# A linear-recurrence attention followed by a PReLU layer: second part block by block, states per 64 tokens, one buffer split, and a static plan with new durations

## The chip, the cores and the metric

One core of a Trainium2 chip. The metric is the device time of one execution in microseconds (us), as the median of the timed runs.

## The reference, cut to what matters

```python
# part 1: batch 4, heads 8, sequence 768, head size 48; for each (b, h):
mag = sqrt(a_re**2 + a_im**2);  scale = minimum(mag, 0.999) / (mag + 1e-6)
for t in range(768):                        # complex decay, real input
    S = (a_re + 1j * a_im)[t, :, None] * scale * S + k[t][:, None] * v[t]
    y[t] = (q[t][:, None] * S.real).sum(0)
# part 2: x is y with the heads side by side, (3072, 384)
h = x @ w_in                                # 384 -> 2048
g = maximum(h, 0) + alpha * minimum(h, 0)
out = g @ w_out                             # 2048 -> 384
```

The first part is done in 24 units of 128 tokens (6 per batch), all heads together. Inside a unit, pairs of tokens are met by levels: the level of h multiplies the second h tokens of each stretch of 2h by the first h. What reaches a unit from earlier tokens comes through a state.

## The kernel before

The program's order of instructions is fixed while it is built. Each piece of work is a generator that yields steps (engine, estimated duration, what it waits for, which buffers it takes). A small planner runs the generators against these durations and puts out the instructions in the order in which they would start. The tasks have dates: a unit of attention is due at `DUE_0 + RATE * u`, the first gates run between `G0`, `G1` and `G2`, the weights are spread from `W_FROM` to `W_TO`. On the chip each engine follows that order, and where an instruction is not ready the engine waits.

```python
class Plan:
    HOP, DRAIN, SLACK, LAND, RATE = 0.06, 0.2, 0.4, 2.0, 200.0
    ...
            now = min(t for t, _ in ready) + 0.3      # choice window
            t, task = min(((t, k) for t, k in ready if t <= now), key=lambda x: (not x[1][1][5], x[1][2]))

R = {name: Ring(n) for name, n in dict(               # buffers of the plan
    KQ=3, PP=1, T=2, V=2, W=2, KT=1, St=2, yT=1, xT=2, g=3, ot=2, wtmp=1,
    lv=2, misc=1, y=1, h=2, o=1).items()}             # the last row is PSUM
sizes = [1, 1] + [MC] * ((NU - 4) // MC) + [1, 1]     # blocks of part 2, in 128 tokens; MC = 2

def mlp(m):                                           # one block of part 2
    for f in range(NF):                               # 16 groups of 128 features
        for kk in range(NK):                          # 3 products
            e = yield PE(n * 1.68e-3, ("x", m), ("w_in", f), takes=() if kk else (R["h"],))
            if kk == 0:
                p = ps.tile([P, MT], F32, tag="h", name="ps_h", bufs=2)[:, 0:n]
            nc.tensor.matmul(p, lhsT=w_in_sb[:, kk, f * P:(f + 1) * P], rhs=xT[:, kk], ...)
        ...                                           # ScalarE: relu, VectorE: + alpha part
    for c in range(sizes[m]):                         # then all outputs, one 128 tokens at a time
        for f in range(NF):
            if f == 0:
                p = ps.tile([P, DM], F32, tag="o", name="ps_o")
            nc.tensor.matmul(p, lhsT=G[f][:, cols], rhs=w_out_sb[:, f], ...)

def to_f32(dst, parts, scales, *key):                 # weights arrive as 64-bit floats
    ta = yield ACT(n, ("raw", *key), takes=(R["wtmp"],))
    tmp = work.tile([P, 2] + list(dst.shape[1:]), F32, tag="wtmp", name="wtmp", bufs=1)
    top, rest = tmp[:, 0], tmp[:, 1]
    ...                                               # 2 ScalarE, 5 VectorE steps
    for i, r in enumerate(parts):                     # ps_w: identity products add top and rest
        ...
    R["wtmp"].put(e)

def half_rows():                                      # v re-sorted by level, in DRAM
    for i, h in enumerate(KINDS):
        for n in range(HP):
            ...
            nc.sync.dma_start(dst, src)               # outermost count of src: 64 / h per unit

# in unit(): levels 1, 2, ... 64, then one state per unit
LEVELS = [1 << i for i in range(7)]
...
t = ps.tile([D2, H, D], F32, tag="misc", name="ps_kv")
for n in range(H):
    nc.tensor.matmul(t[:, n], lhsT=KT[:, n], rhs=V[:, n // 2, ...], ...)
```

`D2` is 96 (real and imaginary part of 48), `P` is 128 and `HC` is 64. PSUM is full in both kernels. With each tile in pieces of 2 KB per partition to itself, the tiles take eight: before, lv 2, misc 1, y 2, h 2, o 1; after, lv 2, misc 1, y 2, h 1, o 2. The Trainium skill, "PSUM — Partial Sum Buffer", section "PSUM: the matmul accumulator", gives eight banks of 2 KB. In this change the second output tile is paid for by joining the two tiles of ps_h into one.

Of the kernel before, what the change touches and what calls it, by code (L numbers as in the profile page):

```python
# [15 lines left out]
P = 128  # L16
# [19 lines left out]
class Plan:  # L36
# [4 lines left out]
    HOP = 0.06  # L41
    DRAIN = 0.2
    SLACK = 0.4
    LAND = 2.0
    RATE = 200.0

    def __init__(self):
        self.busy, self.done, self.tasks = {}, {}, []

# [7 lines left out]
    def _ready(self, e, engine):  # L57

        if e[1] in (engine, None):
            return e[0]  # L60
        return e[0] + self.HOP + self.DRAIN * (e[1] == "PE") + self.SLACK * (engine == "PE")

# [16 lines left out]
    def run(self):  # L79
        while self.tasks:  # L80
# [5 lines left out]
            now = min(t for t, _ in ready) + 0.3  # L86
# [17 lines left out]
def kernel(  # L104
# [46 lines left out]
    LEVELS = [1 << i for i in range(7)]  # L151
# [51 lines left out]
    def POOL(n, *after):  # L203
        return "POOL", 0.12 + n * 1.9e-3, after, (), 0, False

    def PE(us, *after, takes=()):
        return "PE", us, after, takes, 0, False

    def DMA(kb, *after, takes=(), engine="SP"):
# [3 lines left out]
        KQ=3, PP=1, T=2, V=2, W=2, KT=1, St=2, yT=1, xT=2, g=3, ot=2, wtmp=1,  # L213
        lv=2, misc=1, y=1, h=2, o=1).items()}
# [12 lines left out]
    nc.gpsimd.memset(decays_sb[:, :, TL - 1], 0.0)  # L227

    def gates(b, c0, c1):
# [6 lines left out]

        def small(k, *after):

            return POOL(k, *after) if k <= SMALL else DVE(k, *after)

        def on(k):
            return nc.gpsimd if k <= SMALL else nc.vector
# [56 lines left out]
        for o, (p, w) in enumerate(((y, -1.0), (x, 1.0), (y, 1.0))):  # L299
            tu = yield ACT(2 * N, tx, t)  # L300
            nc.scalar.activation(U3[:, o], p.rearrange("p (n l) -> p l n", l=L), AF.Copy, scale=w)  # L301
        at = 0
        while at < TL - 2:
# [20 lines left out]
        def product(dst, u, w, m, k, t):  # L324

            m = m[:, 0:4 * k].rearrange("p (a c n) -> p a c n", a=2, c=2)
            yield small(2 * k, t)
            on(2 * k).tensor_tensor(out=m, in0=w[:, 1::-1].unsqueeze(2).to_broadcast([P, 2, 2, k]), in1=pairs_of(u), op=ALU.mult)  # L328
# [25 lines left out]
        def three(dst, re_im, t):  # L354

            yield ACT(re_im.free_size(), t)
            nc.scalar.copy(dst[:, 1:3], re_im)
            t = yield ACT(re_im.free_size() // 2, t)
            nc.scalar.activation(dst[:, 0], re_im[:, 1], AF.Copy, scale=-1.0)
            return t  # L360
# [6 lines left out]
        t = yield POOL(10, t)  # L367
        if first:
            nc.gpsimd.memset(run[:, 0, :, 0], 1.0)
            nc.gpsimd.memset(run[:, 1, :, 0], 0.0)  # L370
        else:
            nc.gpsimd.tensor_copy(run[:, :, :, 0], carry)
# [3 lines left out]
        if not last:  # L376
            yield POOL(10, t)
            nc.gpsimd.tensor_copy(carry, run[:, :, :, nr])
# [6 lines left out]
        for o in range(2):  # L385
            yield POOL(2 * k, t)
            nc.gpsimd.tensor_tensor(out=m, in0=blk[:, :, 0:Rn - 1],
               in1=turned(runs, o).unsqueeze(2).to_broadcast([P, 2, Rn - 1, rows]), op=ALU.mult)
            t = yield POOL(k)
            nc.gpsimd.tensor_tensor(out=offv[:, o, 1:Rn], in0=m[:, 0], in1=m[:, 1], op=ALU.add)  # L390
# [4 lines left out]
        yield POOL(nb, t)  # L395
        nc.gpsimd.tensor_tensor(out=n2[:, 0], in0=n2[:, 0], in1=n2[:, 1], op=ALU.add)
        yield POOL(nb)
        nc.gpsimd.tensor_scalar(out=n2[:, 0], in0=n2[:, 0], scalar1=-0.5, scalar2=1.5, op0=ALU.mult, op1=ALU.add)
        t = yield POOL(2 * nb)
        nc.gpsimd.tensor_tensor(out=off, in0=off, in1=n2[:, 0].unsqueeze(1).to_broadcast([P, 2, nb]), op=ALU.mult)  # L400
# [59 lines left out]
    def to_f32(dst, parts, scales, *key):  # L460

        n = 2 * DM
        ta = yield ACT(n, ("raw", *key), takes=(R["wtmp"],))
        raw = raws.pop(key)
        lo, hi = raw[:, :, :, 0], raw[:, :, :, 1]
        tmp = work.tile([P, 2] + list(dst.shape[1:]), F32, tag="wtmp", name="wtmp", bufs=1)
        top, rest = tmp[:, 0], tmp[:, 1]
        top_u, dst_u = top.bitcast(U32), dst.bitcast(U32)
        nc.scalar.activation(top, hi.bitcast(F32), AF.Abs)
        tl = yield ACT(n, ta)  # L470
        nc.scalar.activation(rest, lo, AF.Copy, scale=2.0 ** -52)

        yield DVE(n // 2, ta)
        nc.vector.tensor_scalar(out=top, in0=top, scalar1=F64_SMALL, scalar2=None, op0=ALU.max)

        yield DVE(n // 2)
# [7 lines left out]
        yield DVE(n // 2)  # L484
# [3 lines left out]
        nc.vector.tensor_tensor(out=rest, in0=rest, in1=top, op=ALU.mult)  # L488
        for i, r in enumerate(parts):
# [9 lines left out]
        R["wtmp"].put(e)  # L499
# [102 lines left out]
    def unit(u):  # L602
# [18 lines left out]
        def mask_out(name, t, n, e):  # L621

            takes = (R[name],)
            if name in by_row or name == HC:
                e = yield ACT(HP * n if name == HC else HP * name + 100, e, takes=takes)
# [4 lines left out]
            if name == HC:  # L630
                nc.scalar.copy(a, t)
            elif name in by_row:
# [49 lines left out]
        for h in LEVELS[1:-1]:  # L682
# [11 lines left out]
        h = HC  # L694
        e, t = yield from meet(h, lambda n: KQ[:, 1, n, 0:HC], second(h), HC, k_, q_)

        if c + 1 < NCH:
            k_ = yield DVE(H * HC, e)
            step(1, h)
        if c:  # L700
            q_ = yield DVE(H * HC, e)
            step(0, h)
        yield from mask_out(h, t, HC, e)


        before, known = state.pop(b, (None, None))
        if c + 1 < NCH:
            for i in range(2):
                e = yield PE(0.34, k_, takes=(R["misc"],))
                t = ps.tile([P, HP, D2], F32, tag="misc", name="ps_kt")  # L710
                for p in range(4):
                    nc.tensor.transpose(t[:, p], KQ[:, 1, 4 * i + p], ident[:D2, :D2])
                e = yield ACT(HP * D2, e, takes=() if i else (R["KT"],))
                if i == 0:
                    KT = work.tile([P, H, D2], F32, tag="KT", name="KT", bufs=1)
                nc.scalar.copy(KT[:, 4 * i:4 * i + 4], t)
                R["misc"].put(e)
            e = yield PE(1.32, e, ("V", u), takes=(R["misc"],))
            V = L["V"]
            t = ps.tile([D2, H, D], F32, tag="misc", name="ps_kv")  # L720
            for n in range(H):
                nc.tensor.matmul(t[:, n], lhsT=KT[:, n], rhs=V[:, n // 2, (n % 2) * D:(n % 2 + 1) * D],  # L722
                                 start=True, stop=True)
            R["KT"].put(e)
            if before is None:
                s_ = yield ACT(H * D, e, takes=(R["St"],))
                St = work.tile([D2, H, D], F32, tag="St", name="St", bufs=2)
                nc.scalar.copy(St, t)
            else:
                s_ = yield DVE(H * D, known, takes=(R["St"],))  # L730
                St = work.tile([D2, H, D], F32, tag="St", name="St", bufs=2)
                nc.vector.tensor_tensor(out=St, in0=before, in1=T[:, :, TL - 2:TL - 1].to_broadcast([D2, H, D]),
                                        op=ALU.mult)
                s_ = yield DVE(H * D, e)
                nc.vector.tensor_tensor(out=St, in0=St, in1=t, op=ALU.add)
            R["misc"].put(s_)
            state[b] = St, s_
            R["T"].put(s_)
        else:
            R["T"].put(q_)  # L740

        g, cg = group_of[u]
        for s in range(2):
            for part in range(2):
                names = [("own", 0), ("own", 1)] + [(h, 0) for h in LEVELS]
                e = yield PE(0.58, ("V", u), *(made if not (s or part) else ()),
# [5 lines left out]
                for name, own in names[5 * part:5 * part + 5]:  # L752
                    for e_ in range(2):
                        for i in range(2):
# [6 lines left out]
                                             start=(name == "own" and not own), stop=(name == HC and c == 0))  # L761
            if c:
                e = yield PE(0.58, q_, known)
                for i in range(2):
# [148 lines left out]
```

## Time and profile before

| | before |
|---|---|
| time, median of 4 runs (range) | 1106.28 us (1105.12 to 1107.64) |
| span of the profiled run, mean granted clock of TensorE | 1103.6 us, 0.895 |
| first matmul of part 2 | 227.5 us |
| end of the weights' conversion (start of its last product) | 237.7 us |
| last attention product (ps_y) | 998.7 us |

TensorE is the busiest engine by far, so I keep its account throughout as **lost time**: at time t, t minus what all matmuls issued by then would last at full speed. Durations at full speed come from dense stretches of the traces: ps_h 0.220 us for 256 tokens and 0.110 for 128, ps_o 0.324, ps_lv 0.038, ps_y 0.0155, ps_w 0.324, ps_kt 0.083, a ps_kv of whole height 0.083 and of 64 rows 0.047, a state product 0.072 and with half the columns 0.032. Lost time is idle time and low clock together, and is good to about 2 us. Before, the work is 792 us and 312 us are lost by the end of the span.

### The profile page before, as it was taken

What the parts mean: (1) busy time and instruction counts of PE and PEld (TensorE: products, weight loads), DVE (VectorE), ACT (ScalarE), POOL (GpSimd) and SP (SyncE); (2) the same over time, 40 slices, a digit from 0 to 9 for tenths busy, and PEclk for the clock granted to TensorE, in tenths of its full rate; (3) what the DMA queues carried; (4) which work ended last, traced back from release to release, by engine and by line L of the source; (5) the groups of instructions that cost most, each with busy time, mean ns of one, the idle gap of its engine ahead of it and who ended that gap; (6) DMA issues with size and microseconds to landing.
All of it is one profiled execution on the core that took longest, in us unless ns stands there. A gap on an engine that the chain in (4) does not pass through costs nothing.

```text
span 1103.6 us, 23784 instructions
## 1 busy us (share of the span) xinstructions
PE 921.2 (83%) x9952; PEld 647.9 (59%) x9952; DVE 731.6 (66%) x1114; ACT 501.2 (45%) x949; POOL 145.2 (13%) x367
## 2 busy tenths in 40 slices
PE   1453675599978888998897999998989999999998
PEld 0121343376757566676476666685666666877676
DVE  5376789667966587677765877697658765761122
ACT  4362664365625464465244634562546342442122
POOL 5113002400050004000310031003100320000000
PEclk9556667599969899998988999999989989999999
DMA  5784789069726880686338664945393339501000
GB/s 165 207 186 125 174 216 277 7 171 169 172 93 166 180 215 22 191 169 140 119 120 159 157 154 120 216 108 144 127 203 77 97 101 171 133 10 30 7 15 15
DMA packets 210179, 147.05 MB, mean 133 GB/s; under 512 B 71704, under 2 KB 201880, under 8 KB 210072
## 3 DMA queue, kind: packets, MB, share of 16 engines
q1 hardware_dynamic: 210072, 145.53, 54.5%
q8 instruction: 78, 1.28, 0.5%
q14 instruction: 29, 0.24, 0.1%
HBM read 117.19 MB, written 47.97 MB: 150 GB/s over the span
## 4 chain that ended last, share of the span: by engine, by line
PE 60%; DVE 14%; ACT 8%; POOL 7%; issue 5%; SPq 3%; DMA 2%; DVEq 0%; ACTq 0%; POOLq 0%
PE ps_o L829 21%; PE ps_h L810 18%; PE ps_lv L617 6%; PE ps_y L759 5%; POOL tmp L328 3%; PE ps_kv L722 2%; POOL blk L330 2%; DVE tmp L328 2%; PE ps_y L767 2%; SPq L544 2%; DVE KQ L679 2%; PE ps_lv L660 2%; DVE g L818 2%; ACT tmp L301 2%; ACT g L816 2%
## 5 line engine op out<-in xcount | busy, mean ns | idle before, releaser
L810 PE MATMUL ps_h<-xT,w_in_sb 128*128 128x256 f32 (+1 forms) x1344 | 302.4, 373 | 18.7 <-issue 10.7
L829 PE MATMUL ps_o<-w_out_sb,g 128*128 128x384 f32 x768 | 279.9, 505 | 1.8 <-ACT ot L835 1.8
L810 PEld LDWEIGHTS ps_h<-xT,w_in_sb 128*128 128x128 f32 x1344 | 227.5, 197 | 63.4 <-DVE g L818 21.3
L679 DVE TENSOR_TENSOR KQ<-KQ,T 96x512 f32<-96x512 f32 x280 | 191.6, 693 | 81.7 <-PE ps_lv L617 51.3
L818 DVE SCALAR_TENSOR_TENSOR g<-ps_h,al_sm,g 128x256 f32<-128x256 f32 (+1 forms) x224 | 98.4, 443 | 180.5 <-ACT g L816 179.0
L829 PEld LDWEIGHTS ps_o<-w_out_sb,g 128*128 128x128 f32 x768 | 139.4, 192 | 83.7 <-ACT ot L835 3.1
L816 ACT ACTIVATE g<-ps_h,al 128x256 f32<-128x256 f32 (+1 forms) x224 | 98.9, 443 | 140.1 <-PE ps_h L810 139.2
L617 PEld LDWEIGHTS ps_lv<-KQ,W 96*64 96x64 f32 x1920 | 70.5, 144 | 68.4 <-ACT W L685 32.6
L617 PE MATMUL ps_lv<-KQ,W 96*64 96x64 f32 x1920 | 86.4, 234 | 19.9 <-ACT W L685 15.0
L308 POOL TENSOR_TENSOR decays_sb<-decays_sb 128x72 f32<-128x72 f32 (+8 forms) x37 | 16.8, 454 | 586.5 <-DVE decays_sb L308 584.3
L685 ACT COPY W<-KQ 96x512 f32<-96x512 f32 x120 | 74.7, 622 | 36.2 <-DVE KQ L679 35.6
L494 PE MATMUL ps_w<-w_in_sb,ident 128*128 128x512 f32 (+1 forms) x32 | 23.6, 836 | 55.9 <-POOL blk L330 24.7
L617 PE MATMUL ps_lv<-KQ 96*64 96x64 f32 x768 | 36.2, 241 | 32.4 <-ACT A L637 26.0
L780 ACT COPY yT<-ps_y 48x256 f32<-48x256 f32 x96 | 31.1, 368 | 66.6 <-PE ps_y L767 63.7
L301 ACT ACTIVATE tmp<-ab 128x1152 f32<-128x1152 f32 (+2 forms) x27 | 56.5, 2121 | 9.5 <-DVE decays_sb L296 9.4
L617 PEld LDWEIGHTS ps_lv<-KQ 96*64 96x64 f32 x768 | 29.5, 150 | 53.0 <-ACT A L637 34.8
L607 DVE TENSOR_TENSOR KQ<-KQ,PP 96x2048 f32<-96x2048 f32 x24 | 54.7, 2280 | 7.9 <-DMA PP<-phs 4.4
L759 PE MATMUL ps_y<-A,VL 64*48 64x64 f32 x2688 | 48.2, 220 | 5.4 <-issue 5.4
L495 PE MATMUL ps_w<-wtmp,ident 128*128 128x384 f32 (+2 forms) x64 | 43.8, 781 | 8.1 <-DVE wtmp L488 7.9
L637 ACT ACTIVATE A<-ps_lv,rows 128x64 f32<-128x64 f32 x144 | 38.4, 328 | 26.4 <-PE ps_lv L617 25.3
L835 ACT COPY ot<-ps_o 128x384 f32<-128x384 f32 x24 | 11.6, 482 | 84.0 <-PE ps_o L829 83.9
L328 DVE TENSOR_TENSOR tmp<-tmp 128x576 f32<-128x576 f32 (+2 forms) x63 | 43.2, 686 | 6.3 <-ACT tmp L301 5.6
(104 smaller groups left out, 1098.7 us busy)
## 6 DMA issues: line engine op xcount, KB each, us to landing
vsc<-in_v_dram SPq DMA_DIRECT2D x128, 144.0 KB
VL<-vsc SPq DMA_DIRECT2D x24, 768.0 KB
T<-decs SPq DMA_DIRECT2D x48, 384.0 KB
KQ<-in_q_dram SPq DMA_DIRECT2D x48, 192.0 KB
KQ<-in_k_dram SPq DMA_DIRECT2D x48, 192.0 KB
PP<-phs SPq DMA_DIRECT2D x48, 192.0 KB
decs<-decays_sb SPq DMA_DIRECT2D x7, 1152.0 KB
phs<-tmp SPq DMA_DIRECT2D x14, 576.0 KB
```

The lines of the kernel that those rows point to most:

```text
L301: nc.scalar.activation(U3[:, o], p.rearrange("p (n l) -> p l n", l=L), AF.Copy, scale=w)
L328: on(2 * k).tensor_tensor(out=m, in0=w[:, 1::-1].unsqueeze(2).to_broadcast([P, 2, 2, k]), in1=pairs_of(u), op=ALU.mult)
L495: nc.tensor.matmul(p, lhsT=ident, rhs=low, start=False, stop=True)
L607: nc.vector.tensor_tensor(out=KQ, in0=KQ, in1=PP.unsqueeze(1).to_broadcast([D2, 2, H, P]), op=ALU.mult)
L617: nc.tensor.matmul(t[64 * i:64 * i + 64, p], lhsT=weights(4 * i + p), rhs=moving(KQ[:, 0, 4 * i + p]), start=True, stop=True)
L679: nc.vector.tensor_tensor(out=x, in0=x, in1=decays(h)[:, i].unsqueeze(3).to_broadcast([D2, H, n, h]), op=ALU.mult)
L685: nc.scalar.copy(W.rearrange("p n t -> p (n t)").rearrange("p (m h) -> p m h", h=h), halves(KQ[:, 1].rearrange("p n t -> p (n t)"), h)[:, ...
L759: nc.tensor.matmul(o, lhsT=vp[64 * i:64 * i + 64, s, e_ * D:(e_ + 1) * D], rhs=a[:, HC * own:HC * (own + 1)], start=(name == "own" and not ...
L810: nc.tensor.matmul(p, lhsT=w_in_sb[:, kk, f * P:(f + 1) * P], rhs=xT[:, kk], start=(kk == 0), stop=(kk == NK - 1))
L816: nc.scalar.activation(gt, p, AF.Relu, scale=al_1[:, f:f + 1])
L818: nc.vector.scalar_tensor_tensor(out=gt, in0=p, scalar=al_sm[:, f:f + 1], in1=gt, op0=ALU.mult, op1=ALU.add)
L829: nc.tensor.matmul(p, lhsT=G[f][:, cols], rhs=w_out_sb[:, f], start=(f == 0), stop=(f == NF - 1))
```

## The change

The intent: less TensorE work, an even flow between the engines in the second part, a ramp that does not hang on one buffer, and a plan that knows the measured durations. Cut to its core:

```diff
-    LEVELS = [1 << i for i in range(7)]
+    LEVELS = [1 << i for i in range(6)]
-        KQ=3, ... St=2, yT=1, xT=2, g=3, ot=2, wtmp=1,
-        lv=2, misc=1, y=1, h=2, o=1).items()}
+        KQ=3, ... St=3, yT=1, xT=2, g=3, ot=2, top=1, rest=1,
+        lv=2, misc=1, y=1, h=2, o=2).items()}
 # states: two per unit, of 64 tokens each
-            for n in range(H):
-                nc.tensor.matmul(t[:, n], lhsT=KT[:, n], rhs=V[:, n // 2, ...], ...)
+        for n in range(H):
+            for s in range(1 if last else 2):
+                rows = slice(HC * s, HC * (s + 1))
+                nc.tensor.matmul(kv[s][:, n], lhsT=KT[rows, n], rhs=V[rows, n // 2, ...], ...)
 # conversion: one buffer becomes two, the first released early
-        tmp = work.tile([P, 2] + list(dst.shape[1:]), F32, tag="wtmp", name="wtmp", bufs=1)
+        top = work.tile(list(dst.shape), F32, tag="top", name="top", bufs=1)
+        rest = work.tile(list(dst.shape), F32, tag="rest", name="rest", bufs=1)
+        R["top"].put(t)                      # ahead of the identity products
 # first gates: small products on VectorE instead of GpSimd
+        tiny, tiny_engine = (DVE, nc.vector) if b == 0 and first else (POOL, nc.gpsimd)
 # second part: feature f, then the outputs of feature f - 2 for both tiles
-    def mlp(m): ...
+    ps_h = ps.tile([P, 2, MT], F32, tag="h", name="ps_h")        # both halves in 2 KB
+    LAG = 2
+    def features(m, f):
+            ...  p = ps_h[:, f % 2, 0:n]
+    def outputs(m, f, gt, r):
+            ...  sums[c] = ps.tile([P, 512], F32, tag="o", name="ps_o", bufs=2)[:, 0:DM]
+    def all_mlp():
+        made = []
+        for m in range(len(sizes)):
+            for f in range(NF):
+                made.append((m, f, *(yield from features(m, f))))
+                if len(made) > LAG:
+                    yield from outputs(*made.pop(0))
 # plan: durations (some cut), choice window, dates
-            now = min(t for t, _ in ready) + 0.3
+            now = min(t for t, _ in ready) + 0.1
-        return "POOL", 0.12 + n * 1.9e-3, after, (), 0, False
+        return "POOL", 0.4 + n * 2.0e-3, after, (), 0, False
-        return "PE", us, after, takes, 0, False
+        return "PE", us * plan.pace, after, takes, 0, False      # 1.8, then 1.0 from part 2 on
-    DUE_0, RATE, UNIT, LEAD, GATES_US, W_FROM, W_TO, G0, G1, G2, LOAD = 119.0, 28.0, 30.0, 13.0, 18.0, 3.0, 130.0, 16.0, 28.0, 59.0, 59.0
+    DUE_0, RATE, UNIT, LEAD, GATES_US, W_FROM, W_TO, G0, G1, G2, LOAD = 123.5, 33.1, 69.5, 29.6, 26.3, 28.5, 126.3, 6.1, 10.0, 63.2, 54.7
```

## The prediction

> **What bounds the kernel now.** I read the page's busy row and the 40 slices first, then busy time by stretches of 50 us, then the timeline of the last 100 us, then the waits of TensorE, and last the instructions of the tile wtmp. From the page:
>
> ```profile
> PE 921.2 (83%) x9952; PEld 647.9 (59%) x9952; DVE 731.6 (66%) x1114; ACT 501.2 (45%) x949; POOL 145.2 (13%) x367
> PE   1453675599978888998897999998989999999998
> PEclk9556667599969899998988999999989989999999
> ```
>
> TensorE is the busiest engine, but it is loose for the first fifth (digits 1 to 7, clock 5 to 6 tenths). The clock row also stays under 9 here and there later. The stretches give sizes (us: PE busy, PEld, DVE, ACT, POOL, clock, DMA share, GB/s):
>
> ```profile
> 100.00:150.00 50.00, 31.72 (x260) 19.14 (x264) 41.09 (x47) 29.35 (x45) 3.23 (x7) 0.62 0.64 158
> 150.00:200.00 50.00, 26.89 (x260) 14.81 (x259) 40.30 (x60) 23.91 (x38) 11.48 (x26) 0.69 0.86 233
> ...
> 400.00:450.00 50.00, 42.77 (x482) 33.49 (x479) 38.78 (x66) 24.52 (x52) 15.23 (x38) 0.93 0.36 101
> 450.00:500.00 50.00, 50.00 (x539) 35.04 (x539) 34.65 (x50) 28.95 (x51) 0.00 (x0) 1.00 0.75 178
> ...
> 1000.00:1050.00 50.00, 49.39 (x184) 33.53 (x183) 7.74 (x16) 8.56 (x19) 0.00 (x0) 1.00 0.05 16
> ```
>
> Three stages follow. To about 227 us it is a ramp: gates, weight conversion, two attention units; the first matmul of the second part (ps_h) starts at 227.5 us. From there to 1000 us both parts share TensorE. After it only the second part runs, dense. In the middle, stretches rich in ps_h (26.65 us of it in 400 to 450) leave TensorE idle, and those rich in ps_o (21.99 us in 450 to 500) do not.
>
> What full speed is, I take from the tail (start, us, engine, line, operation):
>
> ```profile
> 998.60 10.59 PE L829 MATMUL ps_o<-w_out_sb,g 128*128 128x384 f32 x32
> 1009.02 21.29 PE L810 MATMUL ps_h<-xT,w_in_sb 128*128 128x256 f32 x96
> ...
> 1062.23 1.61 PE L810 MATMUL ps_h<-xT,w_in_sb 128*128 128x128 f32 x12 [0.17 <-DVE g L818]
> 1064.01 1.61 PE L810 MATMUL ps_h<-xT,w_in_sb 128*128 128x128 f32 x12 [0.17 <-DVE g L818]
> ...
> 1089.57 10.49 PE L829 MATMUL ps_o<-w_out_sb,g 128*128 128x384 f32 x32
> ```
>
> A block of 256 tokens costs 21.1 us for ps_h (0.22 us an instruction) and 2 x 10.5 for ps_o. A block of 128 tokens should cost half, 21.1, but takes 24.1 (the ps_o runs start at 1065.46 and 1089.57): two features per 1.78 us where 12 x 0.11 = 1.32 would do, because each pair waits for VectorE. With ten blocks of 256 and four of 128 tokens the second part needs 10 x 42.2 + 4 x 21.1 = 506 us at full speed. One attention unit at full clock, added up from the timeline around 740 us: own products 1.15, seven levels 0.62 each, transposes 0.67, ps_kv 1.32, ps_y 2.32 and state product 1.14, so 10.9 us; 24 units, 262 us. Of the 876 us after 227, I count 752 as work at this speed (506 + some 22.5 x 10.9). The other 124 are idle time (waits of TensorE, 227 to 1000: 67 us) and matmuls under a low clock (the rest, some 55). The longest waits there:
>
> ```profile
> PE ps_lv L617 <- ACT A L637: 19.6, 6, 4.8
> PE ps_h L810 <- issue: 10.7, 2, 5.6
> PE ps_lv L660 <- issue: 5.5, 2, 3.8
> PE ps_lv L617 <- ACT W L685: 5.4, 5, 2.4
> PE ps_y L759 <- issue: 5.4, 1, 5.4
> PE ps_h L810 <- DVE g L818: 4.9, 12, 0.9
> ```
>
> So most are attention matmuls standing at the head of TensorE's order while ScalarE is not done: the plan put them there too early. Only 4.9 us are the second part's own wait.
>
> The ramp is bound by the weights' conversion, 16 pieces from 17.2 to 237.7 us, 13.8 us each, through one buffer (wtmp):
>
> ```profile
> L469 ACT ACTIVATE wtmp<-raw x16: 877/884/924, 17.2 to 227.3; 128x768 f32<-128x768 f32 x16
> L488 DVE TENSOR_TENSOR wtmp<-wtmp x16: 951/959/994, 25.7 to 232.6; 128x768 f32<-128x768 f32 x16
> L495 PE MATMUL ps_w<-wtmp,ident x64: 379/844/1222, 26.7 to 237.7; 128*128 128x384 f32 x32, 128*128 128x512 f32 x16, 128*128 128x256 f32 x16
> ```
>
> **What the Trainium skill says.** "TensorE: Matmul & The Clock Gate", section "HAM oscillation": TensorE idle for longer than a window of some 3.4 us falls back to the half clock. The trace agrees in kind: 0.62 where PE is 32 of 50 us busy, 1.00 where it is 50. So a removed gap also pays in clock. "TensorEngine Tiling (Array Packing)", "Key Properties": different tiles of the array load weights and multiply in parallel. The trace agrees: 56 ps_y matmuls on 64x48 tiles take 0.96 us (17 ns each), 16 of ps_kv on the whole height 1.32 (82 each). "PSUM — Partial Sum Buffer", "PSUM bank collisions raise a hardware error": two engines must not touch one bank in the same partitions at once, at whatever address, so accesses are to be guarded by bank. Before, the two ps_h buffers are separate tiles, and the trace shows TensorE writing one at 1064.01 while VectorE reads the other at 1064.28. No run shows yet what happens when, as after the change, both halves lie in one 2 KB tile.
>
> **The change part by part.**
> (1) States per 64 tokens. Gone per unit: the 64-level's eight products (0.62 us of PE) and its ps_y share (0.9 / 7 per half, two halves: 0.26). The state product becomes two sets of eight matmuls with half the columns, taken as equal to the 1.14 before. ps_kv doubles to 16 matmuls of 64 rows; in pairs on the two row halves I take the same 1.32. So 0.88 x 24 = 21 us less. More: the last unit of each batch now needs transposes and half of ps_kv (about 1.3 x 4 = 5), the first one state product (0.6 x 4 = 2). Net 13 us less of TensorE work. VectorE: 40 level steps of 0.69 go (28 us); state updates rise from 16 to 40 pairs of 0.61 + 0.55 (28 us). Even. ScalarE: 24 copies of 0.37 go (9 us), eight KT copies of 0.48 come (4). DMA: one kind of eight in the gathers of v goes, 16 of 128 issues and an eighth of VL.
> (2) Second part block by block. ps_h of feature f, then ps_o of f-2 for both token tiles. ScalarE and VectorE get 2.64 us per feature where they had 1.32 in the ps_h phase and nothing in the ps_o phase. In the tail the two 128-blocks could fall from 24.1 to 21.1 each: 6 us. If the bank is guarded as one, feature f+1 waits for VectorE on f: 1.2 us for 256 tokens (ScalarE 0.47, VectorE 0.48, hand-overs), which the ps_o pair of 1.32 just covers; for 128 tokens 1.0 against 0.66, so 16 x (0.66 + 1.0) = 27 us a block, 3 worse than now.
> (3) wtmp split in two. The next piece's first step no longer waits for the identity matmuls, 2 to 4 us at the low clock: up to 3 x 16 = 48 us, of which VectorE's load (40 of 50 us in the ramp) lets me count 10 to 30.
> (4) The first gates' small products go from GpSimd to VectorE: the 30 or so small steps between 22.7 and 32.9 us, perhaps 3 us, mostly beside the weights.
> (5) New durations, finer choice (0.1 for 0.3 us), attention due every 33.1 instead of 28. Actual pace was 36.5 us a unit, so the old plan ran too fast and put attention matmuls too early; 33.1 is near the 31.1 us of TensorE work per unit (10.0 + 21.1). I choose one third of the 67 idle us, 22, and with it one third of the 55 lost to clock, 18.
> Sum: 13 (work) + 3 (tail, between +6 and -6) + 20 (ramp) + 22 + 18 = 76, less 16 for new stalls of a plan that still counts two free ps_h buffers: 60. 1106 - 60 = 1046, I say 1045.
>
> **The rivals.**
> A: the shared bank becomes the wait. Where ScalarE or VectorE are late by one op (0.7 us step, 2.5 us gates product), each feature stalls TensorE, and the plan does not know it. At 0.3 us on 160 features of full blocks it costs 48 us, plus 6 in the tail; the gains of (3) and (5) are eaten and the time is 1085 to 1105. For: VectorE is 72% busy in the middle. Against: attention matmuls of 10 us a unit lie between features as well.
> B: TensorE is filled and only its work counts: idle and clock losses fall by two thirds and the ramp by 30. Then 1106 - 13 - 6 - 30 - 80 = 977; I call under 1000 unlikely, because the three gaps of over 5 us with no releaser come once a batch beside the DMA bursts and remain in part.
> C: the ramp does not move, because VectorE and not the one buffer sets it, and the new order only exchanges waits: 13 + 3 + 15 = 31 gained, 1075.
>
> **Range and chances.** B at one in ten, A at one in six, C at one in four, the rest around 1045. That gives 1000 to 1090. Faster by over 2% means under 1084: 0.80. Within 2%: 0.14. Slower: 0.06.
>
> **What would show it.** Right: PE instructions fewer in ps_lv and ps_y, busy time of TensorE some 13 us or more lower; idle before ps_lv in the middle near half; the first ps_h well before 227 us; the last ps_y closer to the end than 104 us; mean clock above 0.895. The bank: ps_h waiting for VectorE's g at every feature in the tail, 128-blocks at 27 us (guarded) or 21 (not). Wrong: first ps_h still near 227, or waits of ps_h on g in the tens of us. If the time is above 1090, A or a plan that fits worse is the cause; below 1000, I underrated what a full TensorE saves in clock.

## The result, and the profile after

| | before | after |
|---|---|---|
| time, median of 4 runs (range) | 1106.28 us (1105.12 to 1107.64) | 1077.37 us (1074.35 to 1078.26) |
| span and mean clock of the profiled run | 1103.6 us, 0.895 | 1072.6 us, 0.922 |
| work of TensorE at full speed | 792 us | 780 us |
| first ps_h, end of conversion | 227.5, 237.7 us | 171.1, 240.0 us |
| last ps_y, and from it to the end | 998.7, 105 us | 939.9, 133 us |
| a block of 128 tokens in the tail | 24.1 us | 28.5 us |

The ratio is 0.9733 (95% interval 0.9711 to 0.9756). Ratios here are the mean time of one kernel's runs over that of the other's of the same rounds, so not quite the ratio of the medians in the table. The change gained 29 us where 61 were predicted. All outputs are right.

The busy row and the two slice rows of the kernel after answer to those of before:

```profile
PE 898.2 (84%) x9984; PEld 624.7 (58%) x9984; DVE 740.9 (69%) x1154; ACT 495.3 (46%) x933; POOL 155.3 (14%) x326
PE   0546554988938978999979989999899999999987
PEclk9956667989869989999989989999899999999999
```

TensorE is busy 23 us less than before. The ramp ends a little earlier, but the twelfth slice (the 3, from 295 to 322 us) shows a hole, and the last two slices, which were 9 and 8, are 8 and 7. The lost time puts sizes to it:

| lost by | before | after | difference made in the stretch |
|---|---|---|---|
| 250 us | 169 | 157 | 12 gained |
| 400 us | 204 | 208 | 16 given back |
| 950 us | 299 | 275 | 28 gained |
| end of the span | 312 | 293 | 5 given back |

With 12 us less work that makes 31, the difference of the two spans. Three places need reading.

**The tail.** The timeline of TensorE in the kernel after (start, us, engine, line, operation): first a block of 256 tokens, then one of 128.

```profile
1007.01 1.45 PE L832 MATMUL ps_o<-w_out_sb,g 128*128 128x384 f32 x4
1008.30 1.52 PE L810 MATMUL ps_h<-xT,w_in_sb 128*128 128x256 f32 x6
...
1037.96 0.94 PE L810 MATMUL ps_h<-xT,w_in_sb 128*128 128x128 f32 x6 [0.20 <-DVE g L820]
1038.73 0.81 PE L832 MATMUL ps_o<-w_out_sb,g 128*128 128x384 f32 x2
1039.74 0.94 PE L810 MATMUL ps_h<-xT,w_in_sb 128*128 128x128 f32 x6 [0.20 <-DVE g L820]
```

At 256 tokens the outputs of one feature (1.45 us) cover ScalarE and VectorE. At 128 tokens they are half as long (0.81 us) and the next feature's first product waits for VectorE to leave the other half: 1.78 us from feature to feature (1037.96 to 1039.74), so 16 x 1.78 = 28.5 us a block. (From the start of one such block to the start of the next it is 28.8 us.)

**The hole at 300 us.** First the stretches of 50 us, with columns PE, PEld, DVE, ACT, POOL, clock, DMA share, GB/s. Kernel before, then after:

```profile
300.00:350.00 50.00, 40.18 (x434) 31.07 (x433) 36.62 (x58) 20.01 (x48) 14.32 (x36) 0.83 0.40 117
```

```profile
100.00:150.00 50.00, 30.81 (x336) 18.41 (x336) 43.23 (x53) 32.20 (x42) 2.08 (x3) 0.67 0.77 194
300.00:350.00 50.00, 33.19 (x421) 24.66 (x422) 33.38 (x43) 22.13 (x34) 0.00 (x0) 0.77 0.91 206
400.00:450.00 50.00, 47.10 (x662) 33.52 (x660) 36.50 (x52) 27.25 (x54) 5.47 (x11) 0.98 0.85 196
1000.00:1050.00 50.00, 46.26 (x222) 29.48 (x220) 9.57 (x26) 11.42 (x29) 0.00 (x0) 1.00 0.05 17
```

From 300 to 350 us TensorE is 7 us less busy than before, at a lower clock. The stretch from 400 to 450, loose before (42.77 us at 0.93), is now filled, and that from 1000 to 1050, dense before (49.39 us), is looser by the tail's waits. The ramp (100 to 150) is as loose as it was, with VectorE at 43 of 50 us. What stands at the head in the hole is seen in the timeline of TensorE, the timeline of VectorE and the timeline of the issuing queue, all of the kernel after:

```profile
305.84 1.12 PE L622 MATMUL ps_lv<-KQ 96*64 96x64 f32 x16 [9.43 <-DVE KQ L667]
315.30 2.93 PE L810 MATMUL ps_h<-xT,w_in_sb 128*128 128x256 f32 x6 [7.48 <-DMA xT<-ysc]
```

```profile
305.01 0.69 DVE L667 TENSOR_TENSOR KQ<-KQ,T 96x512 f32<-96x512 f32 x1 [7.72 <-DMA T<-decs]
```

```profile
280.23 13.63 SPq L549 DMA_DIRECT2D vsc<-in_v_dram  x4
293.96 4.58 SPq L583 DMA_DIRECT2D T<-decs  x2
312.25 0.38 SPq L795 DMA_DIRECT2D xT<-ysc  x1
```

Read backwards: TensorE waited 9.4 us for VectorE, which waited 7.7 us for the decays T; their transfer was issued only at 293.96 because the queue was held for 13.63 us by four gathers of v (the 32-token level; the longest took 4.7 us). TensorE then waited 7.5 us for x, behind the same queue.

**The middle.** The waits of TensorE from 240 to 930 us (total, times, longest), before and after:

```profile
PE ps_lv L617 <- ACT A L637: 19.6, 6, 4.8
...
PE ps_h L810 <- DVE g L818: 4.7, 11, 0.9
```

```profile
PE ps_h L810 <- DVE g L820: 20.6, 28, 5.7
PE ps_lv L622 <- DVE KQ L667: 9.4, 1, 9.4
PE ps_h L810 <- DMA xT<-ysc: 7.5, 1, 7.5
PE ps_y L762 <- issue: 6.0, 3, 3.0
```

The wait for ScalarE, the longest before, is gone (1.7 us of it are left). Waits of the second part on VectorE, and the hole's two, came in its place. All waits of TensorE in this window sum to 64.4 us before and 59.2 after: much was exchanged, little removed.

### The profile page after: what moved, and what is told of

Same layout as the page of the kernel before. It is cut to its first block, busy times and chain, and to the rows that moved or that the text cites. A ratio compares the mean times of both kernels' runs of the same rounds, so it can differ in the third digit from the quotient of the medians.

```text
span 1072.6 us, 23983 instructions
## 1 busy us (share of the span) xinstructions
PE 898.2 (84%) x9984; PEld 624.7 (58%) x9984; DVE 740.9 (69%) x1154; ACT 495.3 (46%) x933; POOL 155.3 (14%) x326
## 4 chain that ended last, share of the span: by engine, by line
PE 58%; DVE 18%; ACT 7%; POOL 5%; issue 4%; SPq 4%; DMA 4%; DVEq 0%; ACTq 0%; POOLq 0%
PE ps_h L810 23%; PE ps_o L832 15%; PE ps_lv L622 6%; PE ps_y L755 4%; PE ps_kv L715 3%; DVE g L820 3%; ACT g L818 2%; POOL tmp L332 2%; PE ps_y L762 2%; DVE tmp L413 2%; PE ps_lv L663 2%; SPq L549 2%; DVE ab L293 2%; PE ps_kt L703 1%; ACT tmp L305 1%
## 5 line engine op out<-in xcount | busy, mean ns | idle before, releaser
L810 PE MATMUL ps_h<-xT,w_in_sb 128*128 128x256 f32 (+1 forms) x1344 | 327.1, 373 | 48.8 <-DVE g L820 35.4
L810 PEld LDWEIGHTS ps_h<-xT,w_in_sb 128*128 128x128 f32 x1344 | 221.9, 195 | 158.4 <-DVE g L820 115.0
L832 PE MATMUL ps_o<-w_out_sb,g 128*128 128x384 f32 x768 | 295.2, 498 | 0.5 <-ACT ot L837 0.5
L682 DVE TENSOR_TENSOR KQ<-KQ,T 96x512 f32<-96x512 f32 x240 | 167.0, 702 | 64.2 <-PE ps_lv L622 43.2
L312 POOL TENSOR_TENSOR decays_sb<-decays_sb 128x72 f32<-128x72 f32 (+5 forms) x24 | 8.6, 359 | 525.2 <-DVE decays_sb L312 523.9
L499 PE MATMUL ps_w<-w_in_sb,ident 128*128 128x512 f32 (+1 forms) x32 | 20.6, 735 | 51.0 <-DVE tmp L391 28.7
L332 POOL TENSOR_TENSOR tmp<-blk 128x72 f32<-128x72 f32 (+1 forms) x56 | 31.5, 563 | 124.6 <-ACT blk L363 62.5
L500 PE MATMUL ps_w<-rest,ident 128*128 128x384 f32 (+2 forms) x64 | 39.9, 718 | 8.6 <-DVE rest L492 8.5
L715 PEld LDWEIGHTS ps_kv<-V,KT 64*96 64x96 f32 x704 | 38.1, 177 | 11.3 <-issue 5.4
L715 PE MATMUL ps_kv<-V,KT 64*96 64x48 f32 x704 | 41.2, 262 | 4.0 <-ACT KT L707 4.0
```

The lines of the kernel that those rows point to most:

```text
L332: on(4 * k).tensor_tensor(out=m, in0=w[:, 1::-1].unsqueeze(2).to_broadcast([P, 2, 2, k]), in1=pairs_of(u), op=ALU.mult)
L682: nc.vector.tensor_tensor(out=x, in0=x, in1=decays(h)[:, i].unsqueeze(3).to_broadcast([D2, H, n, h]), op=ALU.mult)
L715: nc.tensor.matmul(kv[s][:, n], lhsT=KT[rows, n], rhs=V[rows, n // 2, (n % 2) * D:(n % 2 + 1) * D], start=True, stop=True)
L832: nc.tensor.matmul(sums[c], lhsT=gt[:, c * P:(c + 1) * P], rhs=w_out_sb[:, f], start=(f == 0), stop=(f == NF - 1))
```

## The experiments

My theory after the result was that the block-by-block order is paid for by the shared 2 KB tile of ps_h, and that the rest (states, buffer, plan) gained less than thought. The rival: the parts have no worth of their own, and the plan's dates fit only the work for which they were chosen. Two more things were in dispute, the hole and the split buffer.

### The parts, undone one at a time in the kernel after

**Old order.** Sixteen features, then the outputs, two tiles of ps_h, one ps_o. Everything else as after.

```diff
-    ps_h = ps.tile([P, 2, MT], F32, tag="h", name="ps_h")
-                p = ps_h[:, f % 2, 0:n]
+                p = ps.tile([P, MT], F32, tag="h", name="ps_h", bufs=2)[:, 0:n]
+        for c in range(sizes[m]): for f in range(NF): ...   # outputs after all features
```

> The changed kernel with the second part's old order (16 features, then 16 outputs per token tile), two ps_h tiles in two banks and one ps_o. My theory: block by block gained nothing where TensorE is dense and lost in the tail, 2 x (28.5 - 24.1) = 9 us; so this kernel takes 1066 to 1078 us, and ps_h waits for VectorE's g about 5 us in the middle, not 22. Rival: block by block made the gain in the middle (ScalarE and VectorE loaded evenly): then 1088 to 1100 us.

Measured: 1069.30 us (1067.75 to 1074.25), ratio 0.9671 (0.9642 to 0.9700). This is 8 us faster than the changed kernel, within what was expected. It is also no more than moving one date makes (below), and the two profiled executions are equally long (1072.4 and 1072.6 us): by 950 us the old order has lost 281 us and the new 275, and in the tail the old order, with 24.1 us a block of 128 tokens, makes this up. So in the rest of the change the new order is no gain; a loss is shown for the tail alone. (One duration of the plan, that of ScalarE's step in part 2, goes with the order in this run, and in the two below that bring the new order into the kernel before.) Waits of TensorE in this kernel, 240 to 930 us:

```profile
PE ps_h L808 <- DVE g L816: 24.4, 20, 8.0
```

That is as much as in the kernel after (20.6), with two separate tiles. Under the new plan, therefore, the wait of ps_h for VectorE in the middle is there without the shared tile too; that it would be 5 us, as expected, was wrong.

**States per 128 tokens.** Seven levels and one state per unit, in the kernel after.

```diff
-    LEVELS = [1 << i for i in range(6)]
+    LEVELS = [1 << i for i in range(7)]
-        KQ=3, ... St=3, ...
+        KQ=3, ... St=2, ...
+        h = HC                                        # level 64 back, one ps_kv and one state
```

> The changed kernel with states per 128 tokens and the 64-level again. Theory: TensorE work rises by the 13 us that the prediction counted and the time by 10 to 16, to 1087 to 1093 us. Rival (VectorE, unchanged in sum by the states, is what the middle waits for): time unchanged within 5 us.

Measured: 1110.04 us (1108.01 to 1114.07), ratio 1.0036 (1.0008 to 1.0063). Undoing a part that takes 12 us of work away costs 33, more than either expectation. But in this kernel ps_h waits once for 19.3 us, until 272.5 us, for the transfer of x. The timeline of its issuing queue shows what stood before that transfer:

```profile
253.09 11.80 SPq L549 DMA_DIRECT2D vsc<-in_v_dram  x5
265.01 3.86 SPq L803 DMA_DIRECT2D xT<-ysc  x1
```

These are gathers of v again, as in the hole at 300 us. By 400 us this kernel has lost 226 us where the kernel after has lost 208. So of the 33 us, 12 are work and some 18 are lost in the first 400 us, where this wait stands; it is not shown that they are the price of the longer states.

**Old plan.** All of the plan's numbers back, the code of the parts as after.

```diff
-            now = min(t for t, _ in ready) + 0.1
+            now = min(t for t, _ in ready) + 0.3
-        return "PE", us * plan.pace, after, takes, 0, False
+        return "PE", us, after, takes, 0, False
-    DUE_0, RATE, UNIT, ... = 123.5, 33.1, 69.5, ...
+    DUE_0, RATE, UNIT, ... = 119.0, 28.0, 30.0, ...
```

> The changed kernel laid out with the old durations, dates and choice window. Theory: the new plan made most of the middle's 20 us, so 1092 to 1105 us. Rival: the plan is worth little, the gain is work and order: 1075 to 1085 us.

Measured: 1155.82 us (1153.71 to 1157.03), ratio 1.0443 (1.0421 to 1.0465). The largest effect of all, and beyond both expectations: 78 us, and the changed code under the old plan is slower than the kernel before by 50.

**One conversion buffer.** `top` and `rest` as one tile again, released after the identity products.

```diff
-        ta = yield ACT(n, ("raw", *key), takes=(R["top"],))
+        ta = yield ACT(n, ("raw", *key), takes=(R["top"], R["rest"]))
-        top = work.tile(list(dst.shape), F32, tag="top", name="top", bufs=1)
+        tmp = work.tile([P, 2] + list(dst.shape[1:]), F32, tag="wtmp", name="wtmp", bufs=1)
+        top, rest = tmp[:, 0], tmp[:, 1]
-        R["top"].put(t)
+        R["top"].put(e)
```

> The changed kernel with the conversion's two buffers released together again, after the identity matmuls. If the buffer bounded the ramp as predicted: the first 250 us lose 10 to 30 us more, time 1085 to 1105. If VectorE (over 40 of every 50 us busy in the changed ramp) bounds it: within the 12 us that a moved date makes, and the conversion ends at 240 us as in both kernels.

Measured: 1087.99 us (1085.64 to 1095.61), ratio 0.9847 (0.9802 to 0.9893). The loss by 250 us is 164 where the kernel after has 157 and before 169: some 6 us of the 12 that the ramp gained go with the split buffer in this comparison, less than the 10 to 30 us that the theory expected. The last product of the conversion starts at 253.3 us and not at 240; in the runs with the new plan and two buffers it starts between 239.9 and 248.1. The 11 us in the final time are no more than moving one date makes, so what the buffer is worth stays open.

### The parts, done one at a time in the kernel before

**Order alone.**

```diff
-                    p = ps.tile([P, MT], F32, tag="h", name="ps_h", bufs=2)[:, 0:n]
+    ps_h = ps.tile([P, 2, MT], F32, tag="h", name="ps_h")
+                p = ps_h[:, f % 2, 0:n]          # features f, outputs of f - 2, two ps_o
```

> The kernel before with the second part block by block, ps_h in one bank and two ps_o, and nothing else of the change; old plan. If the order alone is a loss of about 8 us, as undoing it in the changed kernel gave: 1110 to 1125 us, with ps_h waiting for g over 20 us in the middle. If the order is what needs the new plan (the run with the old plan took 1156): over 1130. If it is a gain: under 1100.

Measured: 1148.80 us (1143.26 to 1156.09), ratio 1.0408 (1.0352 to 1.0464).

```profile
PE ps_h L812 <- DVE g L822: 17.0, 23, 5.6
```

Here, with the old plan, TensorE waits 17.0 us in the middle for VectorE to leave ps_h, where the kernel before waited 4.7. The time is that of the second case, an order that needs the new plan.

**Order alone, two banks.** As the last, but ps_h in two tiles of 2 KB. To make room, the transposes, ps_kv and ps_w give up their own tile and share the two of ps_lv.

```diff
-    ps_h = ps.tile([P, 2, MT], F32, tag="h", name="ps_h")
+                p = ps.tile([P, MT], F32, tag="h", name="ps_h", bufs=2)[:, 0:n]
-            p = ps.tile([P, 512], F32, tag="misc", name="ps_w") ...
+            p = ps.tile([P, 512], F32, tag="lv", name="ps_w", bufs=2) ...    # so ps_kt, ps_kv
```

> The kernel before with block by block alone (1149 us when both halves of ps_h lie in one bank), but ps_h in two banks, which is paid for by letting the transposes, ps_kv and ps_w share the two ps_lv banks. Theory (the loss of 43 us is the wait of every feature for VectorE on the feature before, forced by the one bank): 1110 to 1125 us, in spite of the sharing, and 21 to 22 us a block of 128 in the tail. Rival (the loss is the order that the plan finds, or two outputs open at once): 1140 or more, though the tail is short.

Measured: 1138.20 us (1135.17 to 1140.00), ratio 1.0280 (1.0249 to 1.0311). That is near the rival's figure. The waits of ps_h for VectorE in the middle are gone (17.0 to 0), so under the old plan the shared tile made them; but others grew: attention matmuls wait 29.5 us for VectorE and 34.5 for ScalarE, where they waited 13.2 and 24.1 in the run with one tile, and all waits of TensorE from 240 to 930 sum to 90.6 us against 75.8. The 11 us gained are in the tail, seen in this kernel's timeline:

```profile
1120.72 0.83 PE L811 MATMUL ps_h<-xT,w_in_sb 128*128 128x128 f32 x6
1121.39 0.81 PE L833 MATMUL ps_o<-w_out_sb,g 128*128 128x384 f32 x2
1122.04 0.83 PE L811 MATMUL ps_h<-xT,w_in_sb 128*128 128x128 f32 x6
```

No wait stands in brackets, and a feature takes 1.31 us instead of 1.78: 21 us a block. The shared tile is shown to be the cause of the slow tail. The cost of the order in the middle under the old plan (lost by 950 us: 299 before, 327 and 330 in these two) did not go away with it. Whether the shared tile has no part in that cost stays open, since this run also puts the transposes, ps_kv and ps_w into the tiles of ps_lv, which may have made the new waits.

**New plan alone**, in the kernel before: durations, window and dates.

```diff
-            now = min(t for t, _ in ready) + 0.3
+            now = min(t for t, _ in ready) + 0.1
-    DUE_0, RATE, UNIT, ... = 119.0, 28.0, 30.0, ...
+    DUE_0, RATE, UNIT, ... = 123.5, 33.1, 69.5, ...
```

> The kernel before with the new durations, dates and choice window alone (old order, states per 128). With the order worth -8 and the plan +78 in the changed kernel, the three parts cannot be independent. Theory (the plan is the gain, and needs no other part): 1080 to 1095 us. Rival (the dates only fit the changed work): 1100 or more.

Measured: 1093.51 us (1091.38 to 1099.89), ratio 0.9886 (0.9850 to 0.9922). So the plan is worth 13 us with the old code, as the theory expected. Here too ps_h waits 18.5 us for VectorE in the middle, with two tiles and the old order.

**States per 64 tokens alone**, in the kernel before.

```diff
-    LEVELS = [1 << i for i in range(7)]
+    LEVELS = [1 << i for i in range(6)]
-        ... St=2, ...
+        ... St=3, ...                                 # and two ps_kv per unit
```

> The kernel before with states per 64 tokens alone (old order, old plan). The work is 13 us less, so 1090 to 1096 us if TensorE's work counts as predicted; if the old plan turns it into waits, as with the new order (1149 to 1156): 1103 to 1115.

Measured: 1125.14 us (1123.41 to 1132.55), ratio 1.0175 (1.0136 to 1.0214). With 12 us less of work it is 19 slower, and above both expectations; the verdict against 2% is unclear, but the interval lies above 1. New waits stand in its profile: transposes for ScalarE's copies KT 17.1 us, attention matmuls for VectorE's KQ 16.0.

Together these eight kernels give every combination of order, states and plan, in us:

| | states per 128, old plan | states per 64, old plan | states per 128, new plan | states per 64, new plan |
|---|---|---|---|---|
| old order | 1106 (before) | 1125 | 1094 | 1069 |
| new order | 1149 | 1156 | 1110 | 1077 (after) |

The split buffer and the first gates on VectorE are in four of them: 1069, 1077, 1110 and 1156, and not in the other four. So each step along one of the three directions is compared only where both kernels have them or both have not: the order costs 43 (1106 to 1149) under the old plan and 8 (1069 to 1077) under the new; the states cost 19 (1106 to 1125) in the old surroundings and gain 33 (1110 to 1077) in the new; the plan gains 13 (1106 to 1094, ratio 0.9886) or 78 (1156 to 1077). No part has a worth of its own. The two large effects, 43 and 78 us, stand clear of what one moved date makes (12 us, below); the 8, the 13 and, in part, the 19 and the 33 do not.

### How sharp the plan is

**Old dates only**, with new durations and window.

```diff
-    DUE_0, RATE, UNIT, LEAD, GATES_US, W_FROM, W_TO, G0, G1, G2, LOAD = 123.5, 33.1, 69.5, 29.6, 26.3, 28.5, 126.3, 6.1, 10.0, 63.2, 54.7
+    DUE_0, RATE, UNIT, LEAD, GATES_US, W_FROM, W_TO, G0, G1, G2, LOAD = 119.0, 28.0, 30.0, 13.0, 18.0, 3.0, 130.0, 16.0, 28.0, 59.0, 59.0
```

> The changed kernel with the new durations and choice window but the old dates (units due every 28 us, started 30 us ahead). If the dates make the plan's worth: 1130 to 1160, near the 1156 of the whole old plan. If the durations do: 1080 to 1095.

Measured: 1119.16 us (1118.21 to 1122.66), ratio 1.0114 (1.0089 to 1.0139). This lies between the two expectations. Taken back in this order, 42 of the 78 us between the old and the new plan are the dates and the other 37 the durations and the window; the other order was not run.

**One date two microseconds later, and two earlier.**

```diff
-    DUE_0, ... = 123.5, ...
+    DUE_0, ... = 125.5, ...      # and in the other kernel 121.5
```

> The changed kernel with one date moved by 2 us (first due date 125.5 for 123.5), which changes no work, only the order the plan finds. It measures how much of any difference between variants is the luck of an order. If luck is small: within 4 us of 1077. If the dates are tuned to a lucky order: 1082 to 1110.

> The changed kernel with the first due date 2 us earlier (121.5). With 2 us later it took 1089. If the chosen date is a lucky one among neighbours: 1082 to 1100; if the time only rises with later dates: 1070 to 1079.

Measured: later 1089.39 us (1080.03 to 1091.53), ratio 0.9844 (0.9789 to 0.9899); earlier 1078.21 (1075.97 to 1079.15), ratio 0.9735 (0.9714 to 0.9756). A shift of 2 us in one date, with no other edit, costs 12 in one direction (one of its four executions took only 1080.03) and 1 in the other. Two neighbours do not tell whether the time jumps from date to date or only rises with later ones. So a difference of some 10 us between two kernels with reordered plans is no evidence for a cause by itself. It needs a line in the trace.

### The tail and the hole

**Odd features elsewhere.** In blocks of 128 tokens only one output tile is in use; the free one takes the odd features.

```diff
-                p = ps_h[:, f % 2, 0:n]
+                if sizes[m] == 1 and f % 2 and f > 1:
+                    if f == 3:
+                        odd_of[m] = ps.tile([P, 512], F32, tag="o", name="ps_h1", bufs=2)
+                    p = odd_of[m][:, 0:n]
+                else:
+                    p = ps_h[:, f % 2, 0:n]
```

> In blocks of 128 tokens the odd features from the third on go to the ps_o bank that such a block leaves free, so that neighbouring features lie in two banks. Theory (one bank guarded as one): the tail's blocks fall from 28.5 to about 22 us each and the time by 12 to 15, to 1062 to 1066 us. Rival (ScalarE and VectorE are too slow for 128-token features whatever the bank): the tail stays at 1.78 us a feature, time 1075 to 1079 us.

Measured: 1061.49 us (1060.94 to 1063.38), ratio 0.9591 (0.9570 to 0.9611): 16 us faster than after. Two last blocks of 28.5 us at 21.0 would make 15. With the two-bank run this settles the tail.

**Last two blocks joined.** The other way around the same wait: no blocks of 128 tokens at the end.

```diff
-    sizes = [1, 1] + [MC] * ((NU - 4) // MC) + [1, 1]
+    sizes = [1, 1] + [MC] * ((NU - 2) // MC)
```

> The changed kernel with its last two blocks of 128 tokens joined to one of 256, for which the two outputs cover the wait for VectorE. Theory: 2 x (28.5 - 21.1) = 15 us less, 1060 to 1066 us; the join delays nothing since the second part lags the first by 130 us. Rival: nothing gained, because the block starts later.

Measured: 1066.33 us (1065.23 to 1068.14), ratio 0.9633 (0.9612 to 0.9653): 11 us faster than after.

**The gathers in two.** Each gather of the 32-token level, whose outermost count is 2, is issued as two transfers with outermost count 32. Once in the kernel after, once in the kernel before.

```diff
-                    nc.sync.dma_start(dst, src)
+                    for d_, s_ in [(dst, src)] if src.shape[0] > 2 else [(dst[x], src[x]) for x in range(src.shape[0])]:
+                        nc.sync.dma_start(d_, s_)
```

> The changed kernel with each gather of v for the 32-token level issued as two transfers of 32 rows of tokens in place of one whose outermost count is 2; order of everything else the same. In the changed kernel's trace these four gathers per batch take 4.0 us each of the DMA queue, while the DMA engines run at 36 GB/s, and the decays and x of the next unit come late behind them (TensorE idle 9.4 and 7.5 us at 296 to 315 us). Theory (the ramp's gain is given back behind these gathers): they fall to under 1 us each, the stretch 250 to 400 loses 10 to 20 us less, time 1058 to 1068 us. Rival (VectorE or bandwidth sets that stretch): within 4 us of 1077.

> The same edit in the kernel before. The same queue stalls are in its trace (4 us each, at 106 to 117 and 269 to 280 us), where TensorE lost less. Theory: 3 to 12 us faster than before, so a gain that has nothing to do with the change; rival: none.

Measured: in after 1074.33 us (1072.79 to 1075.53), ratio 0.9729 (0.9707 to 0.9751); in before 1102.28 (1100.25 to 1105.21), ratio 0.9985 (0.9958 to 1.0011), which is within noise. The queue's timeline of the first kernel, and its stretch:

```profile
279.94 6.80 SPq L550 DMA_DIRECT2D vsc<-in_v_dram  x8
288.84 0.82 SPq L584 DMA_DIRECT2D T<-decs  x2
303.81 0.38 SPq L796 DMA_DIRECT2D xT<-ysc  x1
```

```profile
300.00:350.00 50.00, 39.65 (x416) 28.55 (x417) 37.39 (x48) 25.47 (x39) 0.00 (x0) 0.84 0.69 167
```

Twice as many issues hold the queue half as long, T and x are issued 5 and 8 us earlier, and TensorE is 39.65 us busy where it was 33.19. Among its waits from 240 to 400 us the one of 9.4 us, for T, is gone; the one for x is still there, and TensorE only comes to it earlier:

```profile
PE ps_h L811 <- DMA xT<-ysc: 8.5, 1, 8.5
```

So the first half of the hole is shown to come from the gathers, and 7 us less are lost by 400 us. At the end no gain is shown: the median is 3 us lower, as the rival's range has it, but against the kernel before on the same chip the ratio is 0.9729 with the edit and 0.9733 without. In the kernel before the same gathers are there, and splitting them changes nothing. So a transfer that was harmless became a wait through the new order of instructions.

**Both mends.** Odd features elsewhere and the gathers in two, in the kernel after.

> The changed kernel with both edits that helped or did no harm: odd features of one-tile blocks in the free ps_o bank (1061 us alone) and the 32-token gathers split (1074 alone, 3 us). If they add up: 1056 to 1062 us.

Measured: 1057.96 us (1054.59 to 1058.99), ratio 0.9550 (0.9527 to 0.9574), the lowest median of all, 19 us under the kernel after.

**Old order with both mends of its kind**: old order, last two blocks joined, gathers in two.

> The changed kernel with the old order of the second part, the last two blocks joined and the 32-token gathers split: everything but the order has its best known form. If the order is worth nothing in the middle: 1055 to 1063 us, as the best run with it (1058). If block by block helps in the middle once its tail is mended: 1066 to 1075.

Measured: 1059.30 us (1056.21 to 1064.18), ratio 0.9573 (0.9525 to 0.9621). With their tails and the hole mended, old and new order are equal within their ranges, as the first of the two expectations had it.

## Why the prediction was right and wrong

The direction was right, and the time lies in the range. But the sum of 60 measured 31 in the profiled runs. Step (5), the plan, misses the most, 12 of the missing 29 us; the ramp (3) and the tail (2) miss 8 each. By the prediction's own terms:

| term | predicted | measured |
|---|---|---|
| (1) less work of TensorE | 13 | 12 |
| (3) ramp, by 250 us | 20 | 12 |
| (5) less idle time and clock, less new stalls, 250 to 950 us: 22 + 18 - 16 | 24 | 12 |
| (2) tail | 3 | -5 |
| sum | 60 | 31 |

- **(1) held.** 792 to 780 us of work. The pairs of ps_kv on two row halves took 1.56 us for 32 instructions of 64 rows (at 719.63 us) against 1.48 for 16 of the whole height (at 738.29 us before), so nearly as taken.
- **(2) failed in the tail.** I named both cases (21 us if the halves are free of each other, 27 if the bank is guarded as one) and then put a gain of 3 into the sum, half of the free case, though the middle of the two is 0. It is guarded as one: 28.5 us. Three runs show it, each without the shared tile or without blocks of 128 tokens at the end; the runs that part the halves use separate tiles in separate banks, so they do not tell whether the guard goes by tile or by bank. The Trainium skill, "PSUM — Partial Sum Buffer", section "PSUM bank collisions raise a hardware error", which I had quoted, says that accesses are to be guarded by bank, so the guarded case was the one to put into the sum: 8 us of the missing 29. In the middle, under the new plan, the wait is as long with two tiles and the old order (24.4 us) as with the shared one (20.6). So rival A was right in the tail; its 48 us in the middle do not appear. Rival B, a filled TensorE, did not come: 59.2 us of waits are left in the middle.
- **(3) was mis-sized by 8, and then given back.** In the first 240 us VectorE waited 32.5 us for ScalarE's step that opens a piece of the conversion before, and 5.5 us for the two such steps after; with one buffer in the changed kernel it is 9.4, so most of this fall goes with the rest of the change and not with the buffer. VectorE was then simply fuller, 74 of the first 100 us against 59, and the conversion ended at 240.0 instead of 237.7. That is rival C's reason, though the first ps_h moved by 56 us. That came with the new plan: it starts at 185.7 us with the plan alone in the kernel before, and at 227.4 with the order alone. Only 12 us remained by 250 us, some 6 of them with the buffer. From 250 to 400 us 16 were given back; the two waits of 9.4 and 7.5 in the hole are named by the trace, and the split of the gathers confirms how the first came about.
- **(5) failed in kind.** I took the plan as something that removes a third of the idle time. The wait I named fell further than predicted (ps_lv for ScalarE's A: 19.6 to 1.7 us), but other waits took its place and their sum fell by 5 us, not 22. The plan alone is worth 13, and in the changed kernel 78. From 250 to 950 us 12 us are gained; 5 of them are fewer waits, and beside the rest stands the granted clock, 0.94 before and 0.96 after in this stretch. (The means of the whole run, 0.895 and 0.922, also hold the first 50 us, where the clock reads 0.82 and 1.00 while TensorE has hardly begun.)
- **The sum itself failed.** I added parts as if each had a worth. The table of eight kernels shows that it has not: the states alone cost 19, the order alone 43, the plan alone gains 13; added up they would make 1155, and the three together with the buffer and the gates make 1077. The rival theory, that the parts have no worth of their own, holds; that the dates fit only the work for which they were chosen holds in part, since the plan gains 13 in the old code. The theory of the shared tile holds for the tail, and for 17 us of waits under the old plan.
- **Rival C's number came, 1075, partly by luck.** It summed 13 + 3 + 15 = 31, and 31 were gained. Its reason, that the new order only exchanges waits, fits the middle (64.4 to 59.2 us); but its ramp of 0 was 12, its tail of 3 was -5 and its 15 for the rest was 12.
- **Of the signs that were named,** fewer instructions in ps_lv (3456 to 3072; in ps_y they are as many as before), 23 us less busy time, less idle time before ps_lv in the middle (38 to 15 us), an early first ps_h and a higher clock came. The last ps_y did not come closer to the end (133 us against 105): the first part ended 59 us earlier, the whole only 31. And ps_h waited 20.6 us for VectorE in the middle, which had been named as a sign of being wrong. (One reading of the prediction is loose: in the first fifth the clock row has a 9 and a 7 beside its 5s and 6s. Nothing rests on it.)

**What stays open**: why exactly the new plan fits the new work so much better (78 us against 13), and what the rest of the loss in the middle after 400 us is made of. A date moved by 2 us costs up to 12, so single waits, which change from kernel to kernel, do not settle it.

## What to carry to other kernels

Where instructions are put in order by a static plan, judge a change together with a plan made for it: a part tried alone under the old dates can lose where it gains in the whole, and ten microseconds of difference between two orders may be chance. When a second accumulator is paid for by putting a double buffer into one bank, work out the shortest block: the overlap is gone there, and a tile that lies idle in that block can take the other half. After a change of order, look at the issuing queue for transfers that were harmless before.

## What the Trainium skill lacked or had wrong

- "PSUM — Partial Sum Buffer", section "PSUM bank collisions raise a hardware error": the rule of guarding by bank agrees with how these programs ran, but the page has no price for it: 1.78 us for a feature of 128 tokens with both halves in one bank, 1.31 with two. At 256 tokens no cost is seen in the tail; in the middle, under the old plan, ps_h waited 17.0 us with one bank and not at all with two.
- "DMA: Bandwidth & Descriptors", section "Why a DMA increments its semaphore by 16 and not by 1": it says that the number of engines is the largest number up to 16 that divides the slowest dimension that is not 1 of both sides, so 2 for the gathers with outermost count 2. The trace agrees in kind: from 285 to 290 us the DMA share is 0.17, and two issues with count 32 in place of one with 2 made the four gathers' issue 6.80 us instead of 13.63. The section does not say there that such a transfer can hold its issuing queue, so that later transfers start late (T 5 us, x 8 us; with the hold, the four gathers took up to 4.7 us each to issue).
- No page consulted warns how far a fixed order of instructions moves the time: one date shifted by 2 us made 1077 into 1089, with the same instructions in another order.
